# Linear attention and a mixture of experts on one core: another routing for the token groups that finish early

## Chip, cores, metric

The kernel runs on one core of a Trainium2 chip. The metric is the device time of one execution in microseconds (us). Before the change it is 932.23 us, the median of 3 runs (930.57 to 932.40).

## What is computed

For each of 8 batches and 8 heads (576 tokens, head dimension 64) `phi(x)` projects x to 128 features, subtracts the largest absolute value of the row, and joins `exp` and `exp` of the negative. With q and k so transformed the attention is linear:

```python
kv = einsum('bhsf,bhsd->bhfd', k_p, v);  z = sum(k_p, axis=2)
out = einsum('bhsf,bhfd->bhsd', q_p, kv) / (einsum('bhsf,bhf->bhs', q_p, z) + 1e-06)
```

Its 4608 rows of 512 numbers go through a mixture of 8 experts. Each row's logits against `w_gate` pick the first largest expert, the softmax value of that expert is its gate, and the row's result is `gate * (relu(x @ w1[e]) @ w2[e])`. "Routing" is what turns logits into the place of every token: the expert, the token's rank among those of the same expert, and tables with which TensorE later finds which token stands in which place of which block of 128.

## The kernel before

There are 4 groups of two batches (NG), each of 9 tiles of 128 tokens (NC) and 4 units (NPR, two heads each), so 16 units. A unit's key-value products are two halves of 30 matmuls. The loop over units emits half A (the second half of the unit before, then a copy of its sum, `kvT`, L384) and half B (the first half of this unit, then its copy). One product is one slot: unit u has the slots 60u-30 to 60u-1 (A) and 60u to 60u+29 (B). Between products `half` puts what two plans name: loads (L), splits of an input into a high and a low part (S), projections of keys (k) and queries (q), the low parts of the key features (p). A queue feeds one or two further matmuls a slot: folds (f), numerators (n), transposes of the query features (t). The order of these matmuls on TensorE is fixed by `chain`. The other engines get their order from the framework's planner, which starts what is ready by its own estimate of times, the earlier in the program first.

A projection (L268 to L270) fills one of 2 PSUM tiles `ps_proj`; VectorE takes its maximum (L274) and the difference `t` (L275). For queries four transposes (two for the last, short chunk) fill one of 2 PSUM tiles `pt` (pool `ps_tr`, L307), which ScalarE reads twice (L325, L326, or L321, L322). For keys ScalarE makes exponentials and their high part (L295), and VectorE or GpSimd the low part `kl` (L297): GpSimd for the chunks 0, 4 and 6, VectorE for 2 and 8. GpSimd also makes the low parts of the inputs (L240) and of v (L342). The pool `ps_kv` has 2 tiles: the running sum `pk` of a half, the fold `pf` (L393, copied at L403), and the rank product `prk`.

`route` makes the steps of a group's routing. A group g of the first three is routed while group g+1 is computed; the last group is routed in two parts (`final` is False, then True) among the first expert products, where every step stands on VectorE. The steps for the early groups were popped at the products 2, 5 and 9 of each ten, with empty steps (`pause`) between them, from half A of the unit after the group's end on. Their small steps alternate between VectorE and GpSimd (`X = G`): the sum of logits (L642), the maximum (L650), the shift (L653), candidates (L657, L658), the first of them (L661), one-hot rows (L665, copied at L671), the counts (L687, L688). Then the rank product on TensorE (L693 to L699), its masking (L701) and sum (L705), the rank's block and its place in the block (L709, L710, int32 in SBUF, copied by GpSimd at L713, L714). Last come two tables per tile: `sel_p` on VectorE and `sel_h` on GpSimd, 128 x 128 in bf16 (L728), nine of each. After the third group `lead` finds the most frequent expert and its first rows.

Of the kernel before, what the change touches and what calls it, by code (L numbers as in the profile page):

```python
# [19 lines left out]
P = 128  # L20
# [3 lines left out]
E = 8  # L24
# [25 lines left out]
def tile_linear_attention_moe(  # L50
# [70 lines left out]
    iota_pb = const.tile([P, P], BF16, name="iota_pb")  # L121
# [6 lines left out]
    neg1 = const.tile([P, 1], F32, name="neg1")  # L128
    neg_h = const.tile([P, NTILE], F32, name="neg_h")
# [8 lines left out]
    def constants2():  # L138
# [6 lines left out]
        G.tensor_copy(iota_pb, iota_i)  # L145
# [11 lines left out]
        G.tensor_scalar_mul(neg1, part1, -1.0)  # L157
        G.tensor_scalar_mul(neg_h, hbase, -1.0)


    onehot = rt.tile([P, NTILE, E], F32, name="onehot")
    choice = rt.tile([P, NTILE], F32, name="choice")
    before = rt.tile([P, E, E], F32, name="before")
    blk = rt.tile([P, NTILE], F32, name="blk")
    sel_p = rt.tile([P, NTILE, P], BF16, name="sel_p")
    sel_h = rt.tile([P, NTILE, P], BF16, name="sel_h")
    base = rt.tile([P, E], F32, name="base")
    V.memset(base, 0.0)
# [31 lines left out]
    PAUSE, BEGIN = 3, 4  # L200
# [258 lines left out]
    slot, queue, last = [0], [], [""]  # L459
# [17 lines left out]
    def half(products, plan, steps=()):  # L477
# [145 lines left out]
    def pause():  # L623
        pass

    def route(g, lgc, c0, n, final=None):
# [5 lines left out]


        X = V if final is not None else G

# [27 lines left out]
        def one_hot():  # L663
            oh_b = tile_of("oh_b", [P, NC, E], BF16)
            V.tensor_tensor(  # L665
                oh_b,
                iota_em.unsqueeze(1).to_broadcast([P, n, E]),
# [3 lines left out]
            X.tensor_copy(onehot[:, js, :], oh_b)  # L671
            r["base_b"] = sg.tile([P, E], BF16, name="base_b")
            X.tensor_copy(r["base_b"], base)

        def count():
            if final:
                pc = ps_kv.tile([P, E], F32, name="pc", tag="pk")
                T.matmul(pc, ones, r["base_b"], start=True, stop=False)
                for c in range(n):
                    T.matmul(pc, ones, r["oh_b"][:, c, :], start=False, stop=(c == n - 1))  # L680
# [3 lines left out]
        def sum_up():  # L684
            if not final:
                gsum = sg.tile([P, E], F32, name="gsum")
                V.tensor_reduce(gsum, onehot[:, js, :].rearrange("p c e -> p e c"), axis=AX.X, op=ALU.add)  # L687
                X.tensor_tensor(base, base, gsum, op=ALU.add)  # L688

        def count_ranks():  # L690
            oh_b, base_b = r["oh_b"], r["base_b"]
            prk = ps_kv.tile([P, n, E], F32, name="prk", tag="pk")
            T.matmul(prk, ltri, oh_b, start=True, stop=False)  # L693
            for c in range(n - 1):
                m = n - 1 - c
                T.matmul(
                    prk[:, c + 1 :, :], ones, oh_b[:, c : c + 1, :].to_broadcast([P, m, E]), start=False, stop=False
                )
            T.matmul(prk, ones, base_b.unsqueeze(1).to_broadcast([P, n, E]), start=False, stop=True)  # L699
            with tc.high_priority(offset=200 if final is None else 0):  # L700
                V.tensor_tensor(tile_of("rks", [P, NC, E]), prk, onehot[:, js, :], op=ALU.mult)  # L701

        def rank():
            with nc.allow_low_precision("ranks are integers"):
# [594 lines left out]
```

## Time and profile before

| | us |
|---|---|
| median of 3 runs | 932.23 |
| profiled execution, device time | 934.12 |
| its span, first to last instruction | 932.3 |
| TensorE busy (PE) | 894.5 (96%) |
| VectorE (DVE) | 605.1 (65%) |
| ScalarE (ACT) | 594.3 (64%) |
| GpSimd (POOL) | 491.8 (53%) |

The attention runs from 0 to about 430 us, the experts after it. Mean granted clock of TensorE: 0.987. A row of a timeline has the start, the duration, engine, line, operation, output and inputs; brackets tell how long the engine sat idle before it and who ended that.

### The profile page before, as it was taken

Reading aid. Unit: us, or ns where it says so; the run is one execution under the profiler, and the core shown is the slowest. Engines: PE = TensorE matmul, PEld = TensorE weight load, DVE = VectorE, ACT = ScalarE, POOL = GpSimd, SP = SyncE. Lnnn points to the kernel's source line nnn. Section 1 sums busy time; section 2 is a strip of 40 time slices with the busy share of each in tenths; the row PEclk is TensorE's granted clock in tenths of the full one; section 3 lists DMA queues with packets and bytes.
Section 4 is the critical chain, followed back from the end, with each engine's and each line's share of the span. In section 5 each row is a group of like instructions: output and inputs, shape, how many; then the busy total and the mean of one; then the engine's idle time right before and its main releaser. Section 6 shows DMA issues by size and latency. Waiting matters only on the chain. (4 is left out here: it accounts for less than half of the span.)

```text
span 932.3 us, 18390 instructions
## 1 busy us (share of the span) xinstructions
PE 894.5 (96%) x6831; PEld 838.3 (90%) x6831; DVE 605.1 (65%) x1016; ACT 594.3 (64%) x897; POOL 491.8 (53%) x355
## 2 busy tenths in 40 slices
PE   6999999899989999899999999999999999999995
PEld 5999999899979999898889999999999999987883
DVE  6777779777897779768774444444444444457850
ACT  6877777687757777655565555555555555568951
POOL 6766678666776669644344333333333333346641
PEclk9999999899999999899999999999999999999998
DMA  5333332333223332144133143431434634664100
GB/s 148 97 105 105 107 105 70 105 105 98 78 74 106 105 106 69 49 151 131 52 123 122 46 159 114 159 113 46 152 114 157 216 113 149 224 211 127 45 24 15
DMA packets 64620, 102.46 MB, mean 110 GB/s; under 512 B 10702, under 2 KB 28622, under 8 KB 64528
## 3 DMA queue, kind: packets, MB, share of 16 engines
q1 hardware_dynamic: 57136, 80.31, 27.8%
q0 software_dynamic: 6720, 20.80, 7.1%
q8 instruction: 55, 0.90, 0.4%
q14 instruction: 37, 0.30, 0.1%
q10 hardware_dynamic: 672, 0.15, 0.1%
HBM read 136.81 MB, written 20.26 MB: 168 GB/s over the span
## 5 line engine op out<-in xcount | busy, mean ns | idle before, releaser
L997 DVE TENSOR_TENSOR wl<-raw,wh 128x1024 fp32r<-128x1024 f32 x138 | 185.9, 1360 | 135.4 <-ACT wh L996 135.2
L996 ACT CAST wh<-raw 128x1024 fp32r<-128x1024 f32 x184 | 191.2, 1050 | 95.1 <-PE po L1063 66.0
L997 POOL TENSOR_TENSOR wl<-raw,wh 128x1024 fp32r<-128x1024 f32 x46 | 114.4, 2491 | 169.6 <-ACT wh L996 162.1
L415 PE MATMUL pn<-kf,qp 128*128 128x73 f32 x1024 | 161.8, 252 | 0.2
L297 POOL TENSOR_TENSOR kl<-e,kh 128x1024 fp32r<-128x1024 f32 x47 | 112.3, 2389 | 85.4 <-ACT kh L295 78.7
L1041 PE MATMUL pm<-xh,wh 128*128 128x256 f32 x544 | 153.8, 283 | 2.0 <-DVE hl L1049 2.0
L1042 PE MATMUL pm<-xl,wh 128*128 128x256 f32 x544 | 154.3, 284 | 1.0 <-DVE xl L1024 1.0
L1043 PE MATMUL pm<-xh,wl 128*128 128x256 f32 x544 | 154.1, 283 | 0.0
L415 PEld LDWEIGHTS pn<-kf,qp 128*128 128x128 f32 x1024 | 152.6, 191 | 0.8 <-DVE kf L403 0.8
L274 DVE TENSOR_REDUCE mx<-ps_proj 128x4 f32<-128x512 f32 (+1 forms) x160 | 101.2, 632 | 69.0 <-PE ps_proj L270 68.8
L1061 PE MATMUL po<-wh,hh 128*128 128x512 f32 x272 | 109.2, 402 | 0.0
L1041 PEld LDWEIGHTS pm<-xh,wh 128*128 128x128 f32 x544 | 104.2, 192 | 4.9 <-DVE hl L1049 2.4
L1042 PEld LDWEIGHTS pm<-xl,wh 128*128 128x128 f32 x544 | 104.3, 192 | 3.9 <-DVE xl L1024 1.5
L366 PE MATMUL pk<-kh,vl 128*64 128x256 f32 x320 | 106.8, 334 | 0.0
L1062 PE MATMUL po<-wl,hh 128*128 128x512 f32 x272 | 106.7, 392 | 0.0
L1063 PE MATMUL po<-wh,hl 128*128 128x512 f32 x272 | 106.0, 390 | 0.0
L366 PE MATMUL pk<-kl,vh 128*65 128x256 f32 x320 | 105.1, 329 | 0.8 <-DVE kl L297 0.8
L366 PE MATMUL pk<-kh,vh 128*65 128x256 f32 x320 | 105.7, 330 | 0.0
L1043 PEld LDWEIGHTS pm<-xh,wl 128*128 128x128 f32 x544 | 104.3, 192 | 0.0
L275 DVE TENSOR_TENSOR t<-ps_proj,mx 128x512 f32<-128x512 f32 (+1 forms) x160 | 101.2, 634 | 4.6
L240 POOL TENSOR_TENSOR xl<-xr,xh 128x512 fp32r<-128x512 f32 (+2 forms) x63 | 88.6, 1409 | 26.7 <-DVE mx L274 17.4
L268 PE MATMUL ps_proj<-w_hi,xh 128*128 128x256 f32 x288 | 85.8, 298 | 17.3 <-DVE t L275 16.1
(220 smaller groups left out, 2088.9 us busy)
## 6 DMA issues: line engine op xcount, KB each, us to landing
raw<-w SPq DMA_DIRECT2D x184, 512.0 KB
vt<-vv SPq DMA_DIRECT2D x15, 640.0 KB
x_dram<-xrow SPq DMA_DIRECT2D x30, 256.0 KB
xr<-kT SPq DMA_DIRECT2D x15, 320.0 KB
xr<-qT SPq DMA_DIRECT2D x15, 320.0 KB
xr<-kT SPq DMA_DIRECT2D x17, 256.0 KB
xr<-qT SPq DMA_DIRECT2D x17, 256.0 KB
x_dram<-xrow SPq DMA_DIRECT2D x32, 32.0 KB
```

Of the source, the lines that this page charges most:

```text
L274: V.tensor_reduce(mx[:, 0 : 2 * n], psv, axis=AX.X, op=ALU.max, apply_absolute_value=True)
L297: eng.tensor_tensor(kl, e[:, 0:m], kh, op=ALU.subtract)
L366: return T.matmul(st["pk", bb][0:n, hh, :], (vl if j == 1 else vh)[:, 2 * (c + (bb if c == 8 else 0)) + hh, 0:n], (kl if j == 2 else kh)[: ...
L415: m = T.matmul(st["pn"][:, 2 * (c % 3) + hh, :], qp[:, s, s0 + hh, :] if c < 8 else qp[:, s, hh, bb : bb + 2].rearrange("p b q -> p (b q)" ...
L996: A.copy(th, raw[k])
L997: m = (G if k in (POOL_LO if u else POOL_LO0) else V).tensor_tensor(tl, raw[k], th, op=ALU.subtract)
L1041: T.matmul(pm[:, i], th, xh[:, k, :], start=(k == 0), stop=False)
L1042: T.matmul(pm[:, i], th, xl[:, k, :], start=False, stop=False)
L1043: T.matmul(pm[:, i], tl, xh[:, k, :], start=False, stop=(k == KD - 1))
L1061: T.matmul(po, hh[:, i, r], th[:, c], start=(i == j == 0), stop=False)
L1062: T.matmul(po, hh[:, i, r], tl[:, c], start=False, stop=False)
L1063: T.matmul(po, hl[:, i, r], th[:, c], start=False, stop=(i == 1 and j == 3))
```

## The change

The early groups' scratch (logits, candidates, counts, gate sums) goes into one `pt` tile of the transposes' pool, and rank and place into unused columns of the rank product's own tile `prk`. All small steps stand on VectorE; candidates take one operation, the float copies of the one-hot rows, of the ranks and of the running counts are gone (one bf16 tile per count). The tables are made for three tiles at a time: VectorE compares 128 x 384 at once, ScalarE scales the result into `sel_p`, GpSimd multiplies it into `sel_h`. This holds for the last group too, whose scratch stays in SBUF. The steps are booked on slots: logits to gates from 60u+78 in steps of 2, ranks and tables from 60u+106, `lead` from 60u+166 in steps of 3, where u is the unit after the group.

```diff
-    PAUSE, BEGIN = 3, 4
+    TOP_AT, RANK_AT, LEAD_AT = 78, 106, 166
...
-            if i % 10 in (2, 5, 9) and steps:
-                steps.pop(0)()
+            for f in agenda.pop(slot[0], ()):
+                f()
...
-        X = V if final is not None else G
...
+        def room(name, i):
+
+            if final is not None:
+                return tile_of(name, [P, NC, E])
+            r[name] = r["room"][:, i].rearrange("p (c e) -> p c e", e=E)[:, 0:n]
+            return r[name]
+
         def logits():
             assert c0 + n < NC or lgc_done[g] == NPR
+            if final is None:
+                r["room"] = ps_tr.tile([P, 4, P], F32, name="pt")[:, :, 0 : NC * E]
             V.tensor_reduce(
-                tile_of("lg", [P, NC, E]),
+                room("lg", 0),
...
-            X.tensor_tensor(r["lg"], r["lg"], r["lmax"].unsqueeze(2).to_broadcast([P, n, E]), op=ALU.subtract)
+            V.tensor_tensor(r["lg"], r["lg"], r["lmax"].unsqueeze(2).to_broadcast([P, n, E]), op=ALU.subtract)
...
-            cand = tile_of("cand", [P, NC, E])
-            X.tensor_scalar(cand, r["lg"], 0.0, -float(E), op0=ALU.is_ge, op1=ALU.mult)
-            X.tensor_tensor(cand, cand, iota_e.unsqueeze(1).to_broadcast([P, n, E]), op=ALU.add)
+            V.scalar_tensor_tensor(
+                room("cand", 1),
+                r["lg"],
+                0.0,
+                iota_em.unsqueeze(1).to_broadcast([P, n, E]),
+                op0=ALU.is_ge,
+                op1=ALU.mult,
+            )
...
-            X.tensor_copy(onehot[:, js, :], oh_b)
-            r["base_b"] = sg.tile([P, E], BF16, name="base_b")
-            X.tensor_copy(r["base_b"], base)
+            r["base"] = bases[-1]
...
-            prk = ps_kv.tile([P, n, E], F32, name="prk", tag="pk")
+            r["prk"] = ps_kv.tile([P, 4 * P], F32, name="prk", tag="pk")
+            prk = r["prk"][:, 0 : n * E].rearrange("p (c e) -> p c e", e=E)
...
         def rank():
+            r["rank"] = r["prk"][:, P : P + n].bitcast(I32)
             with nc.allow_low_precision("ranks are integers"):
-                V.tensor_reduce(tile_of("rki", [P, NC], I32), r["rks"], axis=AX.X, op=ALU.add)
-
-        def rank_parts():
-            rkb = tile_of("rkb", [P, NC], I32)
-            V.tensor_single_scalar(rkb, r["rki"], 7, op=ALU.arith_shift_right)
-            V.tensor_single_scalar(r["rki"], r["rki"], P - 1, op=ALU.bitwise_and)
-
-        def rank_values():
-            X.tensor_copy(blk[:, js], r["rkb"])
-            X.tensor_copy(tile_of("rkr", [P, NC], bufs=2), r["rki"])
...
-            for eng, dst, by in ((V, sel_p, part1), (G, sel_h, hbase[:, j0 + c : j0 + c + 1])):
-                eng.tensor_scalar(
-                    dst[:, j0 + c, :], iota_pb, r["rkr"][:, c : c + 1], by, op0=ALU.is_equal, op1=ALU.mult
-                )
+                V.tensor_reduce(r["rank"], r["rks"], axis=AX.X, op=ALU.add)
+
+        def rank_low():
+            r["low"] = r["prk"][:, 2 * P : 2 * P + n].bitcast(I32)
+            V.tensor_single_scalar(r["low"], r["rank"], P - 1, op=ALU.bitwise_and)
+
+        def rank_high():
+            V.tensor_single_scalar(blk[:, js], r["rank"], 7, op=ALU.arith_shift_right)
+
+        def select(c, m):
+            sel = sg.tile([P, 3, P], BF16, name="sel", bufs=2)[:, 0:m]
+            V.tensor_tensor(
+                sel,
+                iota_p.unsqueeze(1).to_broadcast([P, m, P]),
+                r["low"][:, c : c + m].unsqueeze(2).to_broadcast([P, m, P]),
+                op=ALU.is_equal,
+            )
+            js = slice(j0 + c, j0 + c + m)
+            A.activation(sel_p[:, js, :], sel, AF.Copy, scale=part1)
+            G.tensor_tensor(
+                sel_h[:, js, :], sel, hbase[:, js].unsqueeze(2).to_broadcast([P, m, P]), op=ALU.mult
+            )
...
-            X.tensor_scalar_add(r["se"], r["se"], 1e-9)
+            r["se"] = r["room"][:, 3, 0:n] if final is None else tile_of("se", [P, NC])
+            V.tensor_reduce(r["se"], r["ex"], axis=AX.X, op=ALU.add)
...
+        return steps[:3] + [gate] + steps[3:] + [sum_up, add_up] + gates, [count_ranks] + ranks + selects
...
-            run(deferred)
-            deferred = route(st["g"] - 1, units[u - 1]["lgc"], 0, NC)
+            first_part, second_part = route(st["g"] - 1, units[u - 1]["lgc"], 0, NC)
+            book(60 * u + TOP_AT, 2, first_part)
+            book(60 * u + RANK_AT, 2, second_part)
             if st["g"] == NG - 1:
-                deferred += lead()
+                book(60 * u + LEAD_AT, 3, lead())
```

## Rows read from the trace of the kernel before

**Rows 1.** The page's second part (40 equal slices of the span): TensorE's busy tenths and the clock granted to it in tenths.

```profile
PE   6999999899989999899999999999999999999995
...
PEclk9999999899999999899999999999999999999998
```

**Rows 2.** Busy time by stretch, whole halves of units: length, then PE, PEld, DVE, ACT, POOL busy (instructions), clock, DMA share, GB/s. The first four are the halves in which group 0 is routed, the last two an A and a B half without routing.

```profile
125.70:138.24 12.54, 11.76 (x113) 11.56 (x112) 10.32 (x18) 7.46 (x13) 7.73 (x7) 1.00 0.43 128
138.24:150.81 12.57, 12.57 (x131) 12.57 (x130) 10.54 (x28) 11.61 (x22) 8.85 (x9) 1.00 0.25 55
150.81:164.06 13.25, 12.07 (x113) 11.66 (x111) 13.10 (x23) 7.10 (x12) 13.14 (x15) 1.00 0.26 88
164.06:182.34 18.28, 15.06 (x121) 14.89 (x120) 13.16 (x26) 12.10 (x22) 11.85 (x7) 0.81 0.36 101
182.34:193.88 11.54, 11.54 (x113) 11.54 (x112) 9.10 (x18) 7.20 (x11) 5.41 (x4) 1.00 0.34 104
193.88:206.20 12.32, 12.32 (x121) 12.32 (x120) 8.67 (x20) 11.84 (x21) 8.71 (x5) 1.00 0.27 72
```

**Rows 3.** ScalarE's timeline: the copies `kvT` that end the B half before the routing of groups 1 and 2 and the B half in which it ends.

```profile
230.04 0.58 ACT L384 COPY kvT<-pk 65x512 f32<-65x512 f32 x1
...
285.72 0.58 ACT L384 COPY kvT<-pk 65x512 f32<-65x512 f32 x1
...
333.45 0.58 ACT L384 COPY kvT<-pk 65x512 f32<-65x512 f32 x1
...
390.25 0.58 ACT L384 COPY kvT<-pk 65x512 f32<-65x512 f32 x1
```

**Rows 4.** What TensorE waited for between 130 and 185 us (total, times, longest), and the matmul at the end of the longest wait, from its timeline.

```profile
PE ps_proj L268 <- DVE t L275: 4.3, 2, 3.2
PE pt L307 <- DVE t L275: 0.8, 1, 0.8
...
168.06 0.55 PE L268 MATMUL ps_proj<-w_hi,xh 128*128 128x256 f32 x1 [3.22 <-DVE t L275]
```

**Rows 5.** VectorE's timeline in the second part of group 0's routing; the last row is a low part of the same form in halves without routing (grouped by line and form, 182.34 to 206.2 us).

```profile
149.64 1.10 DVE L709 TENSOR_SCALAR rkb<-rki 128x9 int32<-128x9 int32 x1
150.78 2.30 DVE L710 TENSOR_SCALAR rki<-rki 128x9 int32<-128x9 int32 x1
...
153.82 0.77 DVE L297 TENSOR_TENSOR kl<-e,kh 128x512 fp32r<-128x512 f32 x1
...
161.48 5.55 DVE L297 TENSOR_TENSOR kl<-e,kh 128x1024 fp32r<-128x1024 f32 x1
...
L297 DVE TENSOR_TENSOR kl<-e,kh 128x1024 fp32r<-128x1024 f32 x1 | 1.2, 1226 | 0.0
```

**Rows 6.** GpSimd's timeline beside it.

```profile
149.44 1.27 POOL L240 TENSOR_TENSOR xl<-xr,xh 128x512 fp32r<-128x512 f32 x1
150.68 2.37 POOL L297 TENSOR_TENSOR kl<-e,kh 128x1024 fp32r<-128x1024 f32 x1
...
153.56 7.29 POOL L728 TENSOR_SCALAR sel_h<-iota_pb,rkr,hbase 128x128 bf16<-128x128 bf16 x9
160.82 2.39 POOL L297 TENSOR_TENSOR kl<-e,kh 128x1024 fp32r<-128x1024 f32 x1
163.18 2.76 POOL L240 TENSOR_TENSOR xl<-xr,xh 128x512 fp32r<-128x512 f32 x2
```

**Rows 7.** Groups by line and form: count, busy us, mean ns, idle before. The last row is the view of one line: shortest, median and longest in ns.

```profile
L728 DVE TENSOR_SCALAR sel_p<-iota_pb,rkr,part 128x128 bf16<-128x128 bf16 x31 | 9.6, 326 | 0.0
L446 DVE TENSOR_TENSOR xrow<-pn,rec 128x384 f32<-128x384 f32 x48 | 26.7, 556 | 1.4
L658 POOL TENSOR_TENSOR cand<-cand,iota_p 128x72 f32<-128x72 f32 x3 | 1.0, 337 | 0.2
L240 POOL TENSOR_TENSOR xl<-xr,xh 128x512 fp32r<-128x512 f32 x32 | 41.2, 1288 | 1.8 <-ACT xh L239 1.8
L642 DVE TENSOR_REDUCE lg<-lgc 128x72 f32<-128x576 f32 x3 | 3.8, 1258 | 0.0
...
L443 DVE TENSOR_SCALAR rec<-pn x48: 146/155/167, 42.5 to 432.1; 128x6 f32<-128x6 f32 x48
```

**Rows 8.** Turns without routing, from TensorE's and ScalarE's timelines: the first transpose of a query piece and the second reading of the piece before it (two pairs), then the first product of a new half and the copy of the half before.

```profile
195.20 0.27 PE L307 MATMUL pt<-ident,t 128*128 128x128 f32 x1
...
195.89 0.59 ACT L326 ACTIVATE qp<-pt 128x512 f32<-128x512 f32 x1
...
201.28 0.27 PE L307 MATMUL pt<-ident,t 128*128 128x128 f32 x1
...
201.27 0.59 ACT L326 ACTIVATE qp<-pt 128x512 f32<-128x512 f32 x1
...
217.66 0.32 PE L366 MATMUL pk<-kh,vh 128*65 128x256 f32 x1
...
217.72 0.58 ACT L384 COPY kvT<-pk 65x512 f32<-65x512 f32 x1 [1.93 <-PE pk L366]
```

**Rows 9.** The copies of the running counts on GpSimd (view of line 673: shortest, median, longest ns, first and last start in us).

```profile
L673 POOL CAST base_b<-base x3: 179/189/189, 16.0 to 257.3; 128x8 bf16<-128x8 f32 x3
```

**Rows 10.** The last group's routing: busy time of 430 to 450 us (columns as in rows 2), and TensorE's only wait in it.

```profile
430.00:450.00 20.00, 17.98 (x142) 16.76 (x142) 19.55 (x90) 10.89 (x24) 4.08 (x7) 1.00 0.13 30
...
440.52 0.39 PE L1041 MATMUL pm<-xh,wh 128*128 128x256 f32 x1 [2.02 <-DVE hl L1049]
```

More of the change, by code (lines that the diff above doesn't have):

```diff
@@ L457, in normalize @@
         )
-    slot, queue, last = [0], [], [""]
+    slot, queue, last, agenda = [0], [], [""], {}
     lgc_done = [0] * NG
@@ L475, in take, with book, half @@
             chain(first[0][2]())
-    def half(products, plan, steps=()):
+    def book(at, pitch, steps):
+        for i, f in enumerate(steps):
+            agenda.setdefault(at + pitch * i, []).append(f)
+    def half(products, plan):
         for i, f in enumerate(products):
@@ L677, in count @@
                 pc = ps_kv.tile([P, E], F32, name="pc", tag="pk")
-                T.matmul(pc, ones, r["base_b"], start=True, stop=False)
+                T.matmul(pc, ones, r["base"], start=True, stop=False)
                 for c in range(n):
-                    T.matmul(pc, ones, r["oh_b"][:, c, :], start=False, stop=(c == n - 1))
+                    T.matmul(pc, ones, onehot[:, j0 + c, :], start=False, stop=(c == n - 1))
                 with tc.high_priority(offset=150):
@@ L685, in sum_up, with add_up @@
             if not final:
-                gsum = sg.tile([P, E], F32, name="gsum")
-                V.tensor_reduce(gsum, onehot[:, js, :].rearrange("p c e -> p e c"), axis=AX.X, op=ALU.add)
-                X.tensor_tensor(base, base, gsum, op=ALU.add)
+                r["gsum"] = r["room"][:, 2, 0:E] if final is None else sg.tile([P, E], F32, name="gsum")
+                V.tensor_reduce(r["gsum"], onehot[:, js, :].rearrange("p c e -> p e c"), axis=AX.X, op=ALU.add)
+        def add_up():
+            if not final:
+                bases.append(rt.tile([P, E], BF16, name=f"base{len(bases)}"))
+                V.tensor_tensor(bases[-1], r["gsum"], r["base"], op=ALU.add)
         def count_ranks():
-            oh_b, base_b = r["oh_b"], r["base_b"]
-            prk = ps_kv.tile([P, n, E], F32, name="prk", tag="pk")
-            T.matmul(prk, ltri, oh_b, start=True, stop=False)
+            r["prk"] = ps_kv.tile([P, 4 * P], F32, name="prk", tag="pk")
+            prk = r["prk"][:, 0 : n * E].rearrange("p (c e) -> p c e", e=E)
+            oh = onehot[:, js, :]
+            T.matmul(prk, ltri, oh, start=True, stop=False)
             for c in range(n - 1):
@@ L696, in count_ranks @@
                 T.matmul(
[L697 removed]
+                    prk[:, c + 1 :, :], ones, oh[:, c : c + 1, :].to_broadcast([P, m, E]), start=False, stop=False
                 )
[L699 removed]
+            T.matmul(prk, ones, r["base"].unsqueeze(1).to_broadcast([P, n, E]), start=False, stop=True)
             with tc.high_priority(offset=200 if final is None else 0):
[L701 removed]
+                V.tensor_tensor(tile_of("rks", [P, NC, E]), prk, oh, op=ALU.mult)
@@ L759, in route @@
                 *selects,
-                all_of(gates),
+                all_of([gate] + gates),
             ]
-        return (
-            BEGIN * [pause]
-            + [logits, top, shift, candidates, pause, pause, first_top, one_hot, pause, sum_up, pause, pause]
-            + [count_ranks, pause, rank, rank_parts, rank_values, pause, pause]
-            + selects
-            + [gate, gate_sum, pause, gate_store]
-        )
-    ON_ACT = (0, 2, 4, 6, 8)
+        return steps[:3] + [gate] + steps[3:] + [sum_up, add_up] + gates, [count_ranks] + ranks + selects
     early_rows = []
@@ L777, in lead @@
         r = {}
-        def pick():
-            base_b = sg.tile([P, E], BF16, name="lbase_b")
-            V.tensor_copy(base_b, base)
-            r["base_b"] = base_b
         def pick_lead():
             pc = ps_kv.tile([P, E], F32, name="pc", tag="pk")
-            T.matmul(pc, ones, r["base_b"], start=True, stop=True)
+            T.matmul(pc, ones, bases[-1], start=True, stop=True)
             top = sg.tile([P, 1], F32, name="top")
```

60 lines of the change are left out of this document (20 added, 40 removed).

## Prediction

> **What bounds the kernel now.** I read the page's slices first. TensorE is at nine tenths or more nearly everywhere, so the time is TensorE's work plus its holes. In the attention the holes come three times, and behind each the granted clock drops to 8 and 9 tenths [rows 1]. They stand where the groups 0, 1 and 2 are routed.
>
> Next I priced them by whole halves of units. Without routing an A half lasts 11.54 us, a B half 12.32, a unit 23.86. The four halves of group 0's routing last 12.54, 12.57, 13.25 and 18.28: 1.00, 0.25, 1.71 and 5.96 too long, together 8.92 [rows 2]. From the copy before to the copy behind, the groups 1 and 2 take 285.72 - 230.04 = 55.68 and 390.25 - 333.45 = 56.80; less two units (47.72) they lose 7.96 and 9.08 [rows 3]. The routing of the early groups costs 25.96 us.
>
> Then the waits. Near group 0 TensorE waits for nothing but VectorE's `t`: 4.3 us for a free `ps_proj` (3.22 in one piece, 1.1 in another) and 0.8 for transposes [rows 4]. The fourth half's 5.96 is thus 3.22 of waiting and 2.7 of slow clock (0.81 over that half, VectorE working beside it) [rows 2, 4].
>
> Why VectorE is late stands in two timelines side by side. L709 and L710, nine integers each, take 1.10 and 2.30 us and end just as GpSimd's operations end (149.44 + 1.27 = 150.71, 150.68 + 2.37 = 153.05). The low part `kl`, 1.23 us undisturbed, takes 5.55: it starts within a GpSimd `kl` and ends a duration after the last of three GpSimd operations in a row, at 165.94 [rows 5, 6]. These three run in a row because nine `sel_h` held GpSimd for 7.29 us before them. Operations of VectorE that read PSUM don't show it: L443 takes 146 to 167 ns in 48 cases [rows 7].
>
> **The change part by part, per early group.**
>
> *The rank's integers.* L709 and L710 go (3.40 us). Their successors read PSUM; by L443 they take 0.16 each and wait for nobody. Bounds: 0.16 (L443) and 2.30 (the wait stays); I take 0.16, since the form of operands is L443's. VectorE -3.1 us.
>
> *The tables.* Nine `sel_p` at 0.326 (2.9 us) become three compares of 128 x 384, by L446 (same size, one operand in PSUM) 0.556 each, 1.7 us: -1.2 on VectorE. Below nothing I see no room: 384 elements were never read faster here. `sel_h` goes from 7.29 us to three products of two inputs. Between 72 elements at 0.337 and 512 at 1.288 [rows 7], 384 come to 1.01, in all 3.0 (bounds 1.0 and 3.9): GpSimd -4.3. ScalarE gets three scalings, by the 512-column copy 0.58 each [rows 3], 1.7 us; in the two undisturbed halves it is busy 19.04 of 23.86 [rows 2], so 4.8 us of idle time hide them. Without that cover the exponentials behind them come up to 1.7 us late.
>
> *The small steps.* About ten operations leave GpSimd, at L658's price 0.34 each 3.4 us. VectorE gets four (shift, candidates, the running count, the gate's epsilon) at about 0.2, +0.8. VectorE in all: -3.1 - 1.2 + 0.8 = -3.5 us, besides the 4.3 us that one `kl` waited. With 7.7 us less before them, GpSimd's three operations no longer meet that `kl`.
>
> *What that gives back.* VectorE stood at 13.10 of 13.25 in the third half and at 17.77 of 23.86 in two undisturbed ones [rows 2]. With the steps: logits to gates are some 3.3 us (L642's 1.26 and ten at 0.2) over 22 slots, at 0.4 us a slot 8.8 us, of which VectorE has 26% idle, 2.2 us. It falls 1.1 us behind. Ranks and tables, 4 x 0.2 + 1.7 = 2.5 us, come over 12 slots (4.7 us, 1.2 idle): another 1.3, less what was made good between. A piece comes every 2.3 us and has two `ps_proj`, so a `t` may come about 2 us late. I leave 0.3 us of waiting a group (0 to 1.2).
>
> *The rank product's matmuls*, ten small ones, stay: the 0.25 of the second half, in which TensorE never waited.
>
> *The rank tile held longer.* `prk` now stays until the third compare, booked two slots before the half ends, and VectorE is then behind. The next half's `pk` needs `prk`'s tile or that of the half before, which is free when `kvT` is copied: 217.72 + 0.58 = 218.30, where TensorE starts the half at 217.66 [rows 8]. Behind a waiting product stands all of TensorE. Between 0 and 0.64, I take 0.6, as the compare will not be done.
>
> *A transpose tile taken.* With one `pt` left, a piece waits for the second reading of the piece before: 195.89 + 0.59 = 196.48 against 195.20, 1.3 us, for the short piece; 201.86 against 201.28, 0.6 us, for the last one [rows 8]. Slot 78 is product 18 of a B half, and the last query piece of a unit (planned at 8, lag 10) is due at that same slot; the next one comes at product 12 of the following A half, after the gates. So at most the 0.6 falls into it. Bounds 0 and 1.9 (both pieces); I take 0.6. VectorE's logits can in turn wait for ScalarE to free the tile, and the candidates for ScalarE's exponential; that is in the 0.3.
>
> Sum per group: 0.25 + 0.3 + 0.6 + 0.6 = 1.75 us in place of 8.65, bounds 0.25 and 4.0. Three groups: 25.96 - 5.25 = 20.7 us (25.2 to 14.0).
>
> *The last group.* VectorE is busy 19.55 of 20 us there and TensorE waits 2.02 for `hl` [rows 10]. About nine small operations go from VectorE; it compares in three operations instead of four of a third of the size, and ScalarE's fifteen operations for five tiles become three. I take 0.7 us off that wait (2.0 to -1.0, where a long compare stands ahead of `hl`).
>
> *The rest.* `lead`, moved to product 16 of its half, reads tables done 48 slots earlier; its matmuls are the same; zero. The counts' first tile is ready from the start; zero.
>
> The profiled execution took 934.12 us (span 932.3): 934.12 - 21.4 = 912.7. The median of the runs lies 1.9 below it: 932.23 - 21.4 = 910.8. I say 911; the case's own range is 906 to 917.
>
> [...] The chip first: a VectorE `kl` of 512, started at 153.82 within the nine one-input `sel_h`, took 0.77 us, hardly delayed; the one beside GpSimd operations of two inputs took 5.55 [rows 5, 6]. [...]
>
> The clock: behind 3.22 us of idleness it fell to 0.81 over the half [rows 2, 4]; behind 1.1 us it stayed at 1.00. [...]
>
> **The rivals.**
>
> *1. The new `sel_h` holds a `kl` up.* Three products in a row are 3.0 us. If a VectorE `kl` meets them, VectorE is 3.0 us late as before, and TensorE loses about that. For: the 5.55 us came in this way [rows 5, 6]. Against: VectorE's `kl` of chunk 2 is planned at product 11, before the tables, the other one long after. 910.8 + 3 x 3.0 = 920; with the clock's 2.7 each 928. Chance 0.15.
>
> *2. The planner pulls the steps ahead.* It placed group 0's `base_b` at 16.0 us, a hundred us before its step [rows 9]. If logits are started as soon as the group's numerators end, they stand where they stood, the first half's 1.0 stays, and the `pt` tile is taken while both short and last piece need it (1.9). Per group 1.0 + 0.25 + 1.9 + 0.6 = 3.75, 11.3 in all: 932.2 - 25.96 + 11.3 - 0.7 = 916.8. Against: the tile must be free. Chance 0.2.
>
> *3. Slower: the one `pt` left starves the transposes.* Logits to gates go through VectorE, ScalarE (the exponential) and VectorE, each in order behind the features' work; ScalarE's readings that free the other tile wait for `t` only through TensorE. If the gates come so late that two pieces per group wait more than about 3 us each, each costs the 5.96 of the present fourth half (wait and clock): 11.9 + 0.85 = 12.8 a group, 932.2 + 3 x (12.8 - 8.65) = 944.6. It decides from 8.65 us of waiting a group. Against: one hold costs at most 1.3 us by rows 8. Chance 0.04.
>
> *4. Nothing comes of it:* the stall is VectorE's load and not its waits, and returns at another slot. Against: 7.7 of the group's VectorE time are waits [rows 5]. 932, chance 0.01.
>
> **How the numbers follow.** Forecast 0.6 (906 to 917), rivals 0.15, 0.2, 0.04, 0.01. The low end is all 25.2 and 2.0 gone, 905; the high end takes in rival 2 and rival 1 without the clock, 922. Left out: part of rival 1, rivals 3 and 4. Faster by over 0.2% (1.9 us, what three runs can tell): 0.95; within it 0.01; slower 0.04.
>
> **What would show it.** Right: no granted clock under 1.00 between 40 and 400 us; halves of at most 13 us; no integer step on VectorE over 0.3 us; no VectorE `kl` over 3 us; waits of TensorE of about 0.6 for `pk` and for `pt`. Rival 1: a `kl` of over 3 us beside `sel_h`. Rival 2: logits directly behind the group's last numerators, transposes waiting for ScalarE. I am wrong if a group still loses over 4 us.

## The result, and the profile after

The changed kernel takes 911.18 us (median of 4 runs, 910.69 to 912.42); the kernel before, on the same chip, 931.78 (4 runs, 930.57 to 932.40). The ratio is 0.978, 95% interval 0.977 to 0.980: 20.6 us faster. The profiled execution of the changed kernel took 910.69 us, with a span of 909.0.

The page's slices of the changed kernel (TensorE's busy tenths and its granted clock), to be held against [rows 1]: the three dips are gone, in TensorE's busy share and in its clock. (The clock's 6 in the first slice lies in the head, before any routing.)

```profile
PE   7999999999999999999999999999999999999994
...
PEclk6999999999999999999999999999999999999998
```

The view of busy time by stretch, over the four halves in which group 0 is routed (columns as in [rows 2]):

```profile
124.56:136.12 11.56, 11.56 (x113) 11.56 (x112) 9.80 (x18) 7.19 (x11) 6.57 (x4) 1.00 0.43 135
136.12:148.50 12.38, 12.38 (x121) 12.38 (x120) 9.92 (x23) 11.83 (x21) 8.76 (x5) 1.00 0.25 73
148.50:160.36 11.86, 11.86 (x122) 11.85 (x120) 11.51 (x30) 7.33 (x14) 6.96 (x5) 1.00 0.40 105
160.36:173.43 13.07, 12.57 (x121) 12.44 (x120) 9.58 (x23) 12.69 (x23) 9.91 (x8) 1.00 0.31 77
```

12.54, 12.57, 13.25 and 18.28 have become 11.56, 12.38, 11.86 and 13.07. Halves without routing last 11.56 and 12.37 here (11.54 and 12.32 before), so the group loses 0.30 + 0.70 = 1.0 us in place of 8.9. VectorE is busy 11.51 of 11.86 us in the third half; that number comes back below.

What TensorE waited for between 130 and 185 us, and the matmul at the end of that wait, against [rows 4]:

```profile
PE pk L360 <- ACT kvT L378: 0.5, 1, 0.5
...
160.99 0.34 PE L360 MATMUL pk<-kh,vh 128*65 128x256 f32 x1 [0.50 <-ACT kvT L378]
```

The 4.3 us for `ps_proj` and the 0.8 for `pt` are gone. What is left is the wait for the copy that frees the other `pk` tile: the product starts at 160.99, while the rank tile is held until the third compare ends at 162.11. VectorE's and GpSimd's timelines, against [rows 5] and [rows 6]:

```profile
144.16 1.29 DVE L643 TENSOR_REDUCE pt<-lgc 128x72 f32<-128x576 f32 x1 [0.39 <-ACT qp L320]
...
157.22 1.21 DVE L291 TENSOR_TENSOR kl<-e,kh 128x1024 fp32r<-128x1024 f32 x1
...
158.82 0.16 DVE L718 TENSOR_SCALAR prk<-prk 128x9 int32<-128x9 int32 x1
159.27 0.16 DVE L721 TENSOR_SCALAR blk<-prk 128x9 int32<-128x9 int32 x1
159.35 0.54 DVE L725 TENSOR_TENSOR sel<-iota_p,prk 128x384 bf16<-128x384 f32 x1
...
161.55 0.56 DVE L725 TENSOR_TENSOR sel<-iota_p,prk 128x384 bf16<-128x384 f32 x1
...
158.36 1.56 POOL L234 TENSOR_TENSOR xl<-xr,xh 128x640 fp32r<-128x640 f32 x1 [2.51 <-ACT xh L233]
159.97 0.83 POOL L733 TENSOR_TENSOR sel_h<-sel,hbase 128x384 bf16<-128x384 bf16 x1
```

The integer steps take 0.16 each beside an `xl` of GpSimd that runs until 159.92; before, the same two took 1.10 and 2.30 and ended with GpSimd's operations. The `kl` is undisturbed at 1.21.

One new wait stands behind the groups, at the lead's product:

```profile
380.10 0.17 PE L818 MATMUL pl<-b,sel_p 128*128 128x3 bf16 x1 [1.36 <-DVE b L807]
```

Where the time went, from the starts of the copies `kvT` in both traces, in us:

| stretch | before | after | difference |
|---|---|---|---|
| start to the first copy | 32.08 | 30.56 | -1.52 |
| four units without routing | 93.62 | 94.00 | +0.38 |
| ten units with the three groups | 264.55 | 242.40 | -22.15 |
| the unit with the lead | 24.45 | 25.86 | +1.41 |
| the last half | 7.21 | 7.22 | +0.01 |
| from the last copy to the span's end | 510.39 | 508.96 | -1.43 |
| span | 932.30 | 909.00 | -23.30 |

The first row is no gain of the change: in the profiles below it lies between 28.8 and 32.1 us, and at 29.05 in `b_slots`, whose head is that of the kernel before. The profiled execution of before lay 2.3 us over its median and that of the changed kernel 0.5 under its own, so the profiles differ by some 2.8 us more than the medians, and the head explains 1.5 of it.

### The profile page after: what moved, and what is told of

Its sections match the earlier page's. It is cut to its first block, busy times and chain, and to the rows that moved or that the text cites. A ratio compares the mean times of both kernels' runs of the same rounds, so it can differ in the third digit from the quotient of the medians.

```text
span 909.0 us, 18311 instructions
## 1 busy us (share of the span) xinstructions
PE 886.0 (97%) x6831; PEld 831.4 (91%) x6831; DVE 586.1 (64%) x996; ACT 594.2 (65%) x894; POOL 465.9 (51%) x303
## 5 line engine op out<-in xcount | busy, mean ns | idle before, releaser
L991 DVE TENSOR_TENSOR wl<-raw,wh 128x1024 fp32r<-128x1024 f32 x138 | 183.4, 1342 | 135.8 <-ACT wh L990 135.8
L991 POOL TENSOR_TENSOR wl<-raw,wh 128x1024 fp32r<-128x1024 f32 x46 | 112.4, 2448 | 171.2 <-ACT wh L990 163.4
L234 POOL TENSOR_TENSOR xl<-xr,xh 128x512 fp32r<-128x512 f32 (+2 forms) x63 | 89.1, 1415 | 31.6 <-DVE mx L268 18.9
L1105 POOL DMA_INDIRECT out<-ob,sidx x41 | 45.2, 1102 | 91.2 <-ACT ob L1103 81.0
```

The source lines that it names most:

```text
L991: m = (G if k in (POOL_LO if u else POOL_LO0) else V).tensor_tensor(tl, raw[k], th, op=ALU.subtract)
```

## The experiments

Twelve kernels, in three lots of four, each lot on one chip beside the kernel before (931.3 to 931.8 us there). The changed kernel did not run beside them; its 911.18 us is the result above. Names that begin with `b` start from the kernel before, those with `a` from the changed one. "Groups" is the time from the fifth to the fifteenth B half's copy, which holds all three early groups, "lead" the unit behind it, both from the run's profile. In `a_both` and `b_slots_lead` the lead's steps are booked earlier and fall into "groups".

| kernel | median us | ratio to before, 95% interval | groups | lead |
|---|---|---|---|---|
| before | 931.8 | | 264.6 | 24.5 |
| after | 911.2 | 0.977 to 0.980 | 242.4 | 25.9 |
| b_ints | 918.7 | 0.985 to 0.989 | 252.5 | 24.6 |
| b_tables | 917.5 | 0.983 to 0.987 | 247.9 | 25.1 |
| b_slots | 923.8 | 0.990 to 0.993 | 246.9 | 31.6 |
| a_pertile | 912.8 | 0.978 to 0.982 | 243.7 | 26.4 |
| a_delay2 | 926.0 | 0.993 to 0.996 | 257.9 | 25.9 |
| a_delay4 | 934.8 | 1.002 to 1.005 | 265.4 | 25.9 |
| a_sbuf | 914.6 | 0.980 to 0.983 | 245.2 | 27.2 |
| a_slots | 919.9 | 0.986 to 0.991 | 251.7 | 27.4 |
| a_both | 917.1 | 0.983 to 0.985 | 251.8 | 22.9 |
| a_rank98_delay2 | 920.0 | 0.986 to 0.989 | 249.5 | 27.3 |
| a_sbuf_delay2 | 914.3 | 0.979 to 0.983 | 245.2 | 25.9 |
| b_slots_lead | 927.9 | 0.992 to 0.996 | 259.7 | 24.3 |

In three of these runs "lead" is 27.2 to 27.4 by TensorE's clock. The lead's product waits 1.4 us in the changed kernel, and the same 1.4 in `a_sbuf`, `a_slots` and `a_rank98_delay2`; but there the clock of the half with it fell to 0.89, and the half lasted 15.56 to 15.76 us in place of 14.22.

### One part alone, three times

**b_ints**: the rank and the inputs of its integer parts in the rank product's PSUM tile, nothing else.

```diff
-V.tensor_reduce(tile_of("rki", [P, NC], I32), r["rks"], axis=AX.X, op=ALU.add)
+r["rank"] = r["prk"][:, P : P + n].bitcast(I32)
+V.tensor_reduce(r["rank"], r["rks"], axis=AX.X, op=ALU.add)
...
-V.tensor_single_scalar(rkb, r["rki"], 7, op=ALU.arith_shift_right)
+V.tensor_single_scalar(rkb, r["rank"], 7, op=ALU.arith_shift_right)
```

> The kernel before, with one part of the change alone: the rank and its two integer parts read the rank product's PSUM tile instead of SBUF. Theory (the run of nine sel_h on GpSimd, 7.3 us, makes the fourth half of a group 5.96 us too long): the two integer steps fall from 3.4 to 0.3 us, the third half's 1.71 shrinks by about 1 us, the fourth half stays near 18 us: 931.8 - 3 x 1 = 929 (926 to 931). [...] Rival B (only the slots matter): 931 to 932.

**b_tables**: one selection per three tiles, as in the changed kernel, with integers, small steps and slots of before. To make room, the constants of the single-tile tables go and the one-hot rows become bf16; in the last group the tables that ScalarE made by itself (`select_a`) go too.

```diff
-selects = [lambda c=c: select(c) for c in range(n)]
+selects = [lambda c=c: select(c, min(3, n - c)) for c in range(0, n, 3)]
```

> The kernel before, with one part of the change alone: one selection per three tiles (compare on VectorE, one scaling on ScalarE, one product on GpSimd), the integers still in SBUF, the small steps still on GpSimd, the slots of before; the constants that only the single-tile tables read go, to make room. Theory (the run of nine sel_h): GpSimd's 7.3 us become three of about 0.83, no VectorE kl over 3 us, the fourth half loses about 5 of its 5.96 us: 931.8 - 3 x 5 = 917 (914 to 921). [...] Rival B (slots): 930 to 932.

**b_slots**: the steps of before, booked at the slots of the changed kernel.

```diff
-PAUSE, BEGIN = 3, 4
+TOP_AT, RANK_AT, LEAD_AT = 78, 106, 166
...
-deferred = route(st["g"] - 1, units[u - 1]["lgc"], 0, NC)
+first_part, second_part = route(st["g"] - 1, units[u - 1]["lgc"], 0, NC)
+book(60 * u + TOP_AT, 2, first_part)
+book(60 * u + RANK_AT, 2, second_part)
```

> The kernel before, with its own steps, tables and scratch, but every step put at the slots of the changed kernel (logits at slot 78, rank product at 106, lead at 166, a step every second slot). Theory (the run of nine sel_h): the run is still there and two slots apart instead of three, so it is rather denser; a VectorE kl behind it still waits over 3 us: 925 to 936. Rival B (the slots are what counts): most of the gain, 912 to 917.

Of what was expected, `b_tables` came out at the theory, `b_ints` 7.3 us under its theory's range (926 to 931), and `b_slots` at neither number. The integers alone give 13.0 us (918.71 against 931.71), the tables alone 14.3, the slots alone 7.9 in which 7.1 more are lost at the lead. In the groups' stretch the three give 12.1, 16.7 and 17.6 us, together 46, where all of the change gives 22.2. They share one stall, and each by itself takes most of it away. (The 17.6 is of one execution; `b_slots_lead` below shows the same steps lose more. The small steps' move to VectorE was not tried alone.)

Here is how. The timelines of `b_ints`, VectorE first, then GpSimd beside it:

```profile
151.84 0.68 DVE L297 TENSOR_TENSOR kl<-e,kh 128x512 fp32r<-128x512 f32 x1
...
159.63 3.26 DVE L297 TENSOR_TENSOR kl<-e,kh 128x1024 fp32r<-128x1024 f32 x1
...
151.68 7.77 POOL L730 TENSOR_SCALAR sel_h<-iota_pb,rkr,hbase 128x128 bf16<-128x128 bf16 x9
159.43 2.38 POOL L297 TENSOR_TENSOR kl<-e,kh 128x1024 fp32r<-128x1024 f32 x1
161.77 3.77 POOL L240 TENSOR_TENSOR xl<-xr,xh 128x512 fp32r<-128x512 f32 x2
```

The nine `sel_h` are all there, and so are the three GpSimd operations in a row behind them. But VectorE's `kl` gets in between the first and the second of the three (159.43 + 2.38 = 161.81, then its 1.1 us, until 162.89), and the two `xl` take 3.77 us in place of 2.76. In the kernel before the same `kl` came behind all three and took 5.55 [rows 5, 6]. Both hold in all three groups; why VectorE gets in after the first here and not there, no run shows. The fourth half, by stretch, in `b_ints` and in `b_tables`:

```profile
161.89:176.32 14.43, 13.22 (x122) 12.66 (x121) 12.22 (x25) 11.56 (x21) 11.25 (x6) 1.00 0.34 85
```

```profile
161.42:173.78 12.36, 12.36 (x121) 12.36 (x120) 8.91 (x21) 11.88 (x22) 9.47 (x6) 1.00 0.37 101
```

14.43 us at a clock of 1.00 in the one (longest wait 0.7), no loss at all in the other, against 18.28 at 0.81. `b_tables` still pays the integers (L703 1.05, L704 2.29 us), yet its `kl` takes 1.25. So at the slots of before it needs both, the integers' 3.4 us and the tables' run, to make VectorE late enough for a wait of 3.2 us; behind that wait the clock was 0.81 over the half.

`b_slots` shows something else besides. Its logits are booked at slot 78 and ran at 131.19 us, some 13 us ahead of those of the changed kernel: the planner pulled them to where they stood before (first half 12.54, as in [rows 2]). Only ranks and tables really moved, from 149 to 156 us. There the integer steps, still in SBUF, took 1.24 and 0.15 us in place of 1.10 and 2.30, and no `kl` stood between the tables and the end of the half: the fourth half lasts 12.32.

### The tables undone, the rest kept

**a_pertile**: per tile one operation on VectorE and one on GpSimd again, in the changed kernel.

```diff
+def select_each(c):
+    for eng, dst, by in ((V, sel_p, part1), (G, sel_h, hbase[:, j0 + c : j0 + c + 1])):
+        eng.tensor_scalar(
+            dst[:, j0 + c, :], iota_pb, r["rkr"][:, c : c + 1], by, op0=ALU.is_equal, op1=ALU.mult
+        )
```

> The changed kernel with the selection alone undone: per tile one compare-and-scale on VectorE and one on GpSimd as before, two tiles to a step, one more small copy on VectorE for the rank as a number; scratch, small steps and slots stay changed. Theory (the run of nine sel_h): GpSimd is held for some 7 us again, its kl and xl come in a row behind it and a VectorE kl waits: 3 to 6 us a group, 911.2 + 3 x 4.5 = 925 (919 to 930). [...]

912.81 us, 1.6 over the changed kernel (1.3 of it in the groups' stretch), where 8 to 19 were expected. GpSimd's timeline, and a `kl` of VectorE:

```profile
158.74 7.10 POOL L730 TENSOR_SCALAR sel_h<-iota_pb,rkr,hbase 128x128 bf16<-128x128 bf16 x9
165.80 2.71 POOL L338 TENSOR_TENSOR vl<-vt,vh 128x1280 fp32r<-128x1280 f32 x1
168.47 2.39 POOL L293 TENSOR_TENSOR kl<-e,kh 128x1024 fp32r<-128x1024 f32 x1
170.81 2.81 POOL L236 TENSOR_TENSOR xl<-xr,xh 128x640 fp32r<-128x640 f32 x2
173.58 2.38 POOL L293 TENSOR_TENSOR kl<-e,kh 128x1024 fp32r<-128x1024 f32 x1
```

```profile
172.64 3.87 DVE L293 TENSOR_TENSOR kl<-e,kh 128x512 fp32r<-128x512 f32 x1
```

GpSimd is held for 7.10 us, works through its backlog without a gap, and a VectorE `kl`, of 0.68 us in `b_ints`, takes 3.87, as the theory had it. But it falls on the turn to the half behind the routing (the copy starts at 172.51), when VectorE has all its steps done, and TensorE loses 0.45 us a group more. The run of nine and a blocked `kl` are not enough for the stall; it depends on how late VectorE already is there.

### VectorE held up by needless sums

**a_delay2** and **a_delay4**: two or four needless sums on VectorE, ahead of the rank.

```diff
+for _ in range(2):
+    V.tensor_reduce(
+        r["prk"][:, 3 * P : 3 * P + n * E].rearrange("p (c e) -> p c e", e=E),
+        lgc[:, c0 : c0 + n].rearrange("p c h e -> p c e h"),
+        axis=AX.X,
+        op=ALU.add,
+    )
```

> The changed kernel with VectorE held up on purpose, once per early group, directly ahead of the rank's first integer step: the logits' sum is made twice more into unused columns of the rank tile, 2 x 1.29 = 2.6 us of VectorE work that nothing reads and that waits for no other engine. Theory now (TensorE has a slack of some 2 us to VectorE, and only lateness beyond it costs time): a group loses 0.5 to 1.5 us, 911.2 + 3 x 1 = 914 (912 to 916). Rival A (in proportion: each us that VectorE is late costs TensorE one): 911.2 + 3 x 2.6 = 919. Rival B (VectorE's load doesn't matter, only its waits for GpSimd): 911.

> The same with four more sums, 4 x 1.29 = 5.2 us per early group, somewhat more than the 4.3 us that one kl waited in the kernel before. Theory now (slack of some 2 us, then a us per us, and the clock's loss once TensorE idles some 3 us): the hole of before comes back without any GpSimd run, 3 to 6 us a group, 911.2 + 3 x 4.5 = 925 (920 to 930). Rival A (in proportion): 911.2 + 3 x 5.2 = 927, and then the run with two sums lies at half of it. Rival B (only waits for GpSimd matter): 911 to 912.

925.95 and 934.84 us; the groups' stretch grows by 5.2 and 7.7 us a group, more than VectorE's delay. TensorE's waits of `a_delay2` in 155 to 180 us, and its fourth half:

```profile
PE pf L387 <- DVE sel L733: 3.0, 1, 3.0
PE pk L360 <- ACT kvT L378: 0.5, 1, 0.5
```

```profile
158.99:176.87 17.88, 14.39 (x121) 14.01 (x120) 11.63 (x29) 13.48 (x24) 12.38 (x8) 0.90 0.41 117
```

It is not `t` that is late here. The first fold `pf` wants the tile that holds the rank, and gets it when the third compare has read it; that compare also waits for the first `sel` buffer, 1.2 us, as GpSimd took a `vl` ahead of the `sel_h`. With four sums the wait is 5.1 us. So the rank tile in the changed kernel has no slack: a delay of VectorE between the rank and the third compare (2.6 and 5.2 us) passes to TensorE whole (3.0 and 5.1), and the clock's drop (0.90 here) comes on top. The theory of a slack of 2 us does not hold at this place, and the "in proportion" of rival A is too low. The "some 3 us" at which `a_delay4`'s theory has the clock fall is not shown as a threshold: 3.22 us gave 0.81 in the kernel before, 3.0 us 0.90 here, and 1.4 us 0.89 in `a_sbuf`. For rival 4 of the prediction this counts: added load on VectorE alone brings the whole loss back, though by another wait.

**a_rank98_delay2**: the rank product eight slots earlier (98 in place of 106), with the two sums.

> The changed kernel with the rank product eight slots earlier (98) and the same 2.6 us of idle sums on VectorE per early group as in the run a_delay2, again ahead of the first integer step. Theory (with the delay it was the rank tile, held until the last compare, that TensorE's pf waited 3.0 us for, not VectorE's lateness itself): eight slots are 3.2 us, the tile is free in time, and a group loses at most 0.5 us more than without the delay: 911.2 - 1.5 + 3 x 0.3 = 910.6 (909 to 913). Rival (VectorE's lateness costs TensorE in proportion, by whichever tile): 920 to 926 as before.

920.0 us, the rival's. The rank tile is no longer waited for; a transpose is, for `t`, 2.5 us in each group. The third halves of the groups 0, 1 and 2 by stretch:

```profile
147.83:162.58 14.75, 12.29 (x125) 12.08 (x124) 14.54 (x34) 8.97 (x17) 8.82 (x7) 1.00 0.48 122
246.52:261.26 14.74, 12.29 (x125) 12.08 (x124) 14.53 (x34) 8.97 (x16) 8.79 (x7) 1.00 0.46 123
345.23:361.06 15.83, 13.37 (x123) 13.16 (x122) 15.00 (x34) 9.07 (x16) 9.21 (x7) 0.89 0.44 121
```

VectorE is busy 14.5 of 14.75 us: with the sums it is the bound in the A half that gets ranks and tables, and in the changed kernel it stands at 11.51 of 11.86 already. What is added there, TensorE waits for in part: the third and fourth halves of group 0 take 26.88 us together, against 25.28 in `a_both` below, whose ranks have the same slots, so 1.6 us for 2.5 of VectorE.

### The scratch back in SBUF

**a_sbuf**: logits, candidates, sums, rank and low part in SBUF, the rest as changed.

```diff
-r["room"] = ps_tr.tile([P, 4, P], F32, name="pt")[:, :, 0 : NC * E]
+r["lg"] = sg.tile([P, NC, E], F32, name="lg")[:, 0:n]
+r["cand"] = sg.tile([P, NC, E], F32, name="cand")[:, 0:n]
+r["few"] = sg.tile([P, E + NC], F32, name="few")
...
-r["rank"] = r["prk"][:, P : P + n].bitcast(I32)
+r["ints"] = sg.tile([P, 2, NC], I32, name="ints")
+r["rank"] = r["ints"][:, 0, 0:n]
```

> The changed kernel with all scratch of the early groups in SBUF again (logits, candidates, group sums, gate sums, rank and low part); tables, small steps on VectorE and slots stay changed. The rank tile is then free after one reading, so TensorE's 0.5 us wait for the next pk goes (3 x 0.5 = 1.5 us). Theory (slack): VectorE's steps wait for GpSimd's kl and xl again, up to 2.4 us each, but spread over 28 slots and made good between them: 909.7 to 915, likeliest 911. Rival A (PSUM scratch is what the gain comes from): 917 to 925.

914.61 us, 3.4 over the changed kernel: within the theory's range, far from rival A's. The 0.5 us for `pk` are gone, as expected, and an integer step waits again (L723, 1.54 us). But the groups' stretch is 2.8 us longer, since without a `pt` tile to wait for, the planner pulls the logits ahead to 133.28 us, and the first half lasts 12.57 us again, with 0.8 us of waiting for a transpose. Rival 2 of the prediction is thus real; what kept it out of the changed kernel is the tile.

**a_sbuf_delay2**: the same with the two sums.

> The run a_sbuf (scratch in SBUF, the rank tile free after its one reading) with the same 2.6 us of idle sums on VectorE per early group. Theory (TensorE's slack to VectorE is about 2 us where no tile is held): a group loses 0 to 1.2 us more than in a_sbuf, 914.6 + 3 x 0.6 = 916.4 (914 to 918.5). Rival (lateness costs in proportion): 914.6 + 3 x 2.6 = 922.4, more where the clock drops too.

914.33 us, and the groups take 245.2 us with or without the sums. This run doesn't tell what it was for: the sums no longer depend on the rank tile, and the planner put them at 143.19 and 144.99 us, into the B half. There 2.6 us of VectorE cost nothing.

### The places

**a_slots**: the changed kernel with logits at slot 45 and ranks at 85, where the kernel before had them.

> The changed kernel with its steps put where the kernel before had them (logits at slot 45, rank product at 85), still two slots apart. Theory (slack; the slots do not matter once the steps are short): 909 to 914, likeliest 911; the rank tile is free long before the half ends or is held across its end, 0 to 0.6 us a group either way. Rival B (the slots are a large part of the gain, as the kernel before with the new slots lost only 3.3 us a group): 915 to 925, with waits of TensorE for pt, since the q pieces' transposes are due while one pt tile is taken.

919.94 us, 8.8 over the changed kernel, rival B's. TensorE's waits of group 0, 125 to 165 us:

```profile
PE pt L301 <- ACT qp L320: 1.2, 1, 1.2
PE pt L301 <- DVE lmax L651: 0.8, 1, 0.8
PE pk L360 <- ACT kvT L378: 0.5, 1, 0.5
PE pf L387 <- DVE sel L725: 0.4, 1, 0.4
```

With one `pt` tile taken while the query pieces need two, transposes wait for ScalarE's reading (1.2) and for the steps themselves (0.8). Scratch in PSUM and the late slots belong together.

**a_both**: two numbers of the changed kernel moved, in the hope of a faster one.

```diff
-TOP_AT, RANK_AT, LEAD_AT = 78, 106, 166
+TOP_AT, RANK_AT, LEAD_AT = 78, 98, 126
...
-book(60 * u + LEAD_AT, 3, lead())
+book(60 * u + LEAD_AT, 8, lead())
```

> The changed kernel with two of its slot numbers moved: the rank product and the selection eight slots earlier (98 in place of 106), so that the rank tile is free before the half ends, and the lead's steps forty slots earlier and eight slots apart (126 and 8, in place of 166 and 3). Theory (the tile that is held is what TensorE still waits for; the lead's steps stand too close together): the 0.50 us waits for pk go (3 x 0.5), so do the 1.4 us for the lead's b and 0.8 us for the gathered rows: 911.2 - 3.7 = 907.5 (906 to 909.5). Rival (the waits only move to another tile or to the logits' pt): 910.5 to 912.

917.09 us, 5.9 slower than the changed kernel and above both numbers. The wait for `pk` went to 0.2, but a transpose waits 0.4 instead; the groups 0 and 1 lose 1.35 us each, not 1.0. The rest is the lead. VectorE's steps of it, and GpSimd's beside them:

```profile
362.41 1.10 DVE L786 TENSOR_TENSOR lcand<-lcand,iota_p 128x8 f32<-128x8 f32 x1
...
364.04 0.14 DVE L788 TENSOR_REDUCE ld<-lcand 128x1 f32<-128x8 f32 x1
364.21 0.14 DVE L789 TENSOR_SCALAR lead_e<-ld 1x1 int32<-1x1 f32 x1
364.29 1.87 DVE L791 TENSOR_SCALAR key<-iota_em,ld 128x8 f32<-128x8 f32 x1
366.07 1.31 DVE L804 TENSOR_SCALAR bl<-choice,ld 128x27 f32<-128x27 f32 x1
367.30 2.37 DVE L792 TENSOR_TENSOR key<-key,iota_p 128x8 f32<-128x8 f32 x1
...
361.91 1.57 POOL L234 TENSOR_TENSOR xl<-xr,xh 128x640 fp32r<-128x640 f32 x1
363.43 2.70 POOL L336 TENSOR_TENSOR vl<-vt,vh 128x1280 fp32r<-128x1280 f32 x1
366.08 1.26 POOL L234 TENSOR_TENSOR xl<-xr,xh 128x512 fp32r<-128x512 f32 x1
367.30 2.34 POOL L291 TENSOR_TENSOR kl<-e,kh 128x1024 fp32r<-128x1024 f32 x1
```

```profile
370.14 0.16 PE L818 MATMUL pl<-b,sel_p 128*128 128x3 bf16 x1 [4.83 <-DVE b L807]
```

Four steps of 8 to 27 elements, 0.14 to 0.22 us each in the changed kernel, take 6.65 us. Each ends within 0.04 us of the GpSimd operation beside it (363.48, 366.13, 367.34, 369.64). The product waits 4.83 us, and the half lasts 21.20 us at a clock of 0.84. In the changed kernel the lead runs where GpSimd is busy 5.94 of 11.64 us. It is the stall of the kernel before, in steps that were left in SBUF.

**b_slots_lead**: `b_slots` with the lead at 130 and eight slots apart.

> The run b_slots (the kernel before with its steps at the slots of the changed kernel) with the lead's steps at 130 and eight slots apart, since there the lead's product waited 3.8 us for VectorE and the half behind it lasted 19.16 us at a clock of 0.82. Theory (these 6.3 us are the lead's, and the new slots by themselves take most of the groups' stall away even with nine single tables on GpSimd): 923.8 - 6.3 = 917.5 (915 to 919.5). Rival (the stall comes back at another place): 921 to 925.

927.88 us; neither number. The lead's product waits 6.8 us here, for the reason just shown (five of its steps take 1.02 to 2.69 us), and in the groups a transpose waits 2.4 us for `t` twice, in halves of 15.69 and 15.50 us at a clock of 0.89. In `b_slots` the same halves, with the same steps, lasted 12.48 and 14.14. One `kl` of VectorE makes the difference; the rows are of groups 0 and 1 in `b_slots`, then in `b_slots_lead`:

```profile
174.07 1.48 DVE L297 TENSOR_TENSOR kl<-e,kh 128x512 fp32r<-128x512 f32 x1 [0.59 <-ACT kh L295]
...
272.71 5.08 DVE L297 TENSOR_TENSOR kl<-e,kh 128x512 fp32r<-128x512 f32 x1 [0.60 <-ACT kh L295]
```

```profile
174.31 5.06 DVE L297 TENSOR_TENSOR kl<-e,kh 128x512 fp32r<-128x512 f32 x1 [0.59 <-ACT kh L295]
...
275.13 5.07 DVE L297 TENSOR_TENSOR kl<-e,kh 128x512 fp32r<-128x512 f32 x1 [0.59 <-ACT kh L295]
```

In the first row VectorE got in between two GpSimd operations, in the others it did not. So the new slots do not remove the blocked `kl`, they move it to the next unit, and what it costs there differs from one execution of the same steps to another. The 917.5 for the slots alone was not reached, and the split of `b_slots` into groups and lead rests on its profile.

## Why the prediction was right, and where not

911.0 was predicted, 911.18 measured. Point by point:

- *The rank's integers*: 0.16 us each predicted and measured; the form of operands decided, as argued from L443 (0.17 and 0.16 in `b_ints`, where nothing but the tile changed).
- *The tables*: compare 0.556 predicted, 0.54 to 0.56 measured; scaling on ScalarE 0.58, measured 0.61; `sel_h` 1.01, measured 0.83.
- *The waits go, so the stall goes*: right, but the chain was told as a sum, and the runs show a coincidence. "These three run in a row because nine `sel_h` held GpSimd" is so, and yet nine `sel_h` in the changed kernel cost 0.45 us a group (`a_pertile`). At the slots of before VectorE must be late by the integers as well.
- *The rank product's matmuls*: 0.25 predicted, 0.30 measured (third half).
- *VectorE's lag*: 0.3 predicted, 0.2 left in the fourth half beside the wait.
- *The rank tile held longer*: 0.6 predicted, 0.50 measured, three times. The upper bound of 0.64 was wrong: it took the wait for the `kvT` copy as the end, and `a_delay2` shows that the next user of the tile, `pf`, can wait longer, 3.0 us.
- *A transpose tile taken*: 0.6 predicted, none measured. VectorE's logits wait 0.39 us for the tile instead, and by the time of the next query piece it is back. At the earlier slots the price is 1.2 + 0.8 us (`a_slots`), near the bound of 1.9.
- Sum per group: 1.75 predicted, 1.0 measured; three groups -20.7 predicted, -22.15 in the profile.
- *The last group*: -0.7 predicted; the wait for `hl` is gone and the last part is 1.43 us shorter. It is gone in `b_ints` and in `a_sbuf` too, and stands at 1.8 in `b_tables`: so it is not the tables. Whether it is VectorE's waits for GpSimd or its number of steps, no run separates, and the 1.43 is no firm figure: with the last part of the kernel before, `b_slots` and `b_slots_lead` need 511.4 and 512.3 us in place of 510.4.
- *The lead*: zero predicted, +1.41 measured. The step that failed is "its matmuls are the same; zero": the product comes three slots behind `find` where it came thirteen behind, and VectorE's steps for it are not done by then; the last ends at 380.05.
- *The rest*: halves without routing are 0.02 to 0.05 us longer, 0.4 us over the first four units, not predicted. Projection matmuls take 282 ns in place of 280 in the kernels that have this; why was not tried.

The errors of the sum, 1.45 too little at the groups and 0.7 at the last group on one side, 1.4 and 0.4 at lead and halves on the other, nearly cancel: -21.8 without the head, where -21.4 was predicted. These are figures of one execution each. By the medians the gain is 20.6, not 21.4, and the base of the prediction, the median of three runs, lay 0.45 over that of four; that cancels in part as well. The agreement to 0.2 us is closer than the working was, and to that extent luck.

Of the signs that were named, the clock of 1.00 in every half from 40 to 400 us, the integer steps under 0.3 (0.16 to 0.17), the `kl` under 3 us (at most 1.73) and the wait for `pk` came true. The halves of at most 13 us did not (13.07 to 13.11, and 14.22 with the lead), nor did a wait for `pt`.

Of the rivals, 1 did not happen: in group 0 VectorE's `kl` ended at 158.43, before the first `sel_h` at 159.97, and no `kl` of VectorE took over 1.8 us in the groups. 2 is a true mechanism (`a_sbuf`, `b_slots`), kept out by the PSUM tile, as its "against" had it. 3's mechanism shows in `a_slots` at 2 us a group. 4 did not happen either, but VectorE's load counts for more than its chance of 0.01 says: with 2.6 us more of it VectorE is the bound in the A half with ranks and tables, and the time goes up (`a_rank98_delay2`).

## What to carry to other kernels

When an engine is late only at one place, undo or do each part of a change alone before crediting any: three parts that each give between half and four fifths of the gain in the groups (12.1, 16.7 and 17.6 of 22.2 us) are three ways around one stall. Scratch in a PSUM tile kept short VectorE steps clear of GpSimd here (0.16 us each beside an `xl`, where in SBUF they took 1.10 and 2.30), but it borrows a tile that something else waits for and it pins the steps in time, so place and lifetime must be chosen with it. Ask of each short chain on VectorE what GpSimd does beside it: in `a_both` four steps of 0.14 to 0.22 us became 6.65 in all.

## What the runs showed of the hardware

- In `a_both` four short VectorE steps on SBUF took 1.10, 1.87, 1.31 and 2.37 us beside GpSimd operations of two inputs, and each ended within 0.04 us of the one beside it; two of the four have one tensor and a scalar per partition as inputs (L791, L804). A reduction and a step of one element beside the same GpSimd `vl` did not take longer (L788, L789, 0.14 each), and with the input in PSUM the integer steps took 0.16 in the changed kernel. Beside one-input `sel_h` the runs differ. In `b_ints` a `kl` of 512 took 0.68, and the first `sel_h` took 1.36 where the others take 0.8, so there it was GpSimd that was held up:

```profile
151.68 1.36 POOL L730 TENSOR_SCALAR sel_h<-iota_pb,rkr,hbase 128x128 bf16<-128x128 bf16 x1
```

By the records that `sel_h` began 0.16 us ahead of the `kl`. In the kernel before, the `kl` of 0.77 [rows 5] ran beside a `sel_h` of 0.86 and one of 0.84, and neither waited for the whole of the other. The prediction took the 0.77 as hardly delayed; the 1.36 shows that a `kl` and a one-input `sel_h` are not always clear of each other. What decides which of the two is held up, no run shows.
- TensorE's clock fell after holes that left it alone at other times. In the kernel before, a wait of 1.1 us left 1.00 over the half and one of 3.22 gave 0.81. A wait of 2.4 to 2.5 us left 1.00 in two groups of `a_rank98_delay2` and gave 0.89 in the third (at a price of 1.1 us) and in two of `b_slots_lead`; 3.0 us gave 0.90 in two groups of `a_delay2` and 0.82 in the third. The lead's wait of 1.36 to 1.37 us, with 1.5 us of products of three columns behind it, left 1.00 in the changed kernel, `a_delay2` and `a_sbuf_delay2`, and gave 0.89 in `a_rank98_delay2`, `a_sbuf` and `a_slots`, at a price of 1.3 to 1.5 us. So in these runs the length of a hole did not decide by itself whether the clock fell, and what else does was not shown.
